# First product of the second layer in seven block products instead of eight

## The chip, the cores and the metric

The kernel runs on one core of one Trainium2 chip. A core has TensorE (matrix products, PE in the rows; its weight loads are listed apart as PEld), VectorE (DVE), ScalarE (ACT), GpSimd (POOL), SyncE (SP) and 16 DMA engines. Each engine works its own instructions in the order of the program and waits for others on semaphores. The metric is the device time of one execution in microseconds; the median of three runs stands for a kernel.

## The reference

Three layers follow each other, in float32: a decayed attention without softmax, a mixture of experts (each of 2304 tokens goes to 2 of 8 experts), and a dense layer, the "second layer" of the change:

```python
def _moe2_ref(x, w_in, w_out):          # x 2304 x 512, w_in 512 x 2048, w_out 2048 x 512
    h = x @ w_in
    relu6 = np.clip(h + 3.0, 0.0, 6.0)
    g = h * relu6 / 6.0
    return (g @ w_out).astype(np.float32)

def reference(**kwargs):
    attn_out = _attn_ref(**attn_kwargs)
    x = attn_out.transpose(0, 2, 1, 3).reshape(B * S, H * D)
    x = _moe_ref(x=x, **moe_kwargs)
    return _moe2_ref(x=x, **moe2_kwargs)
```

## The kernel before

Tokens go in 18 tiles of 128. All products are made in a type of TensorE with fewer bits (`F32R`): every operand is split into a high part, copied by ScalarE, and a low part, the rest, subtracted by VectorE. A product is then three passes, high by high, low by high, high by low, which accumulate in PSUM. `wstep` (L544 and L545) makes the splits of weights, `turn` (L643 to L646) transposes a tile of tokens on VectorE and splits it.

The expert stage (`moe`, about 116 to 564 us) runs in ten sweeps: single, single, six double ones, single, single. A sweep has 8 steps f. Each step makes first products `g1` (L690) into a PSUM tile `ga` or `gb`, ScalarE and VectorE make the high and low part of the hidden tile (L742, L743), and `flush` then issues the second product `g2` (L701) of the step before; so a hidden tile has the length of one step to be made. `w_in` and `w_out` come in a form of 8 bytes per number and are converted in 64 chunks during the sweeps from the third on (`cv_load`, `cv_run`, `cv_store`); the result goes to DRAM (`win`, `wout`). Results of experts go to DRAM (`yd`).

The second layer (`moe2`) takes the tiles in the groups of `GR` (L809): two, two, two, three, three, three, three. A group has 16 steps f, two per weight unit of 256 columns of `w_in` (8 units). A step has 12 matmuls of `g1` with 256 or 384 token columns, the four steps of `glu` (L879 to L882: relu on ScalarE, multiply on VectorE, high part on ScalarE, low part on VectorE), and the `g2` of the step before, three matmuls of 512 columns per tile. After a group's last `g2`, `o_out` (L894) copies its sums out. The split weights of both products are held in SBUF for the whole layer (four buffers `big` per unit).

`x2_prep` makes the tokens of the next group meanwhile: GpSimd gathers two rows of `yd` per token (L818), `x2_mix` adds them with their gates (L826, L827), the tile goes to DRAM and comes back in blocks (L635), and `turn` makes `self.x2`.

The order on each engine is that of the program text. SyncE issues the loads and stores in order, and an issue whose buffer isn't free, or whose data isn't ready, holds those behind it.

Of the kernel before, what the change touches and what calls it, by code (L numbers as in the profile page):

```python
# [64 lines left out]
class K:  # L65
# [437 lines left out]
    def w_load(self):  # L503
# [23 lines left out]
    def w_split(self):
# [4 lines left out]
        h1, l1 = self.big([P, 4, 256], F32R), self.big([P, 4, 256], F32R)  # L532
        h2, l2 = self.big([P, 2, DM], F32R), self.big([P, 2, DM], F32R)
        self.w[n] = (h1, l1, h2, l2)
        for j, (a, b) in enumerate(self.wst.pop(n)):
            s = slice(2 * j, 2 * j + 2)
            self.wq.append((n, h1[:, s], l1[:, s], a))
            self.wq.append((n, h2[:, j], l2[:, j], b))
# [174 lines left out]
    def moe(self, xs0):  # L713
# [3 lines left out]
        for si, sw in enumerate(self.SW):  # L717
# [5 lines left out]
            for f in range(8):  # L723
                n = e * 4 + f // 2
                cur = e * 4 if si in (0, len(self.SW) - 2) else n
                if f % 2 == 0:
                    if self.wsp <= cur + 4:
# [28 lines left out]
                self.prev = (w, fi, [(*s, a) for s, a in zip(subs, accs)], f == 0, f == 7)  # L756
# [52 lines left out]
    GR = [(0, 2), (2, 2), (4, 2), (6, 3), (9, 3), (12, 3), (15, 3)]  # L809
# [19 lines left out]
    def x2_prep(self, gi, f):  # L829

        if gi >= len(self.GR) or f < 0:
            return
        t0, G = self.GR[gi]
        if f == 0:
            self.ys = {}
            self.x2 = (self.act_t([P, 4, 384]), self.act_t([P, 4, 384]))
        step, mix, get, cut = ((0, 2, 4, 5), (3, 4, 6, 8), (3, 4, 6, 8), (2, 4, 6, 8), (3, 3, 5, 7))[min(gi, 4)]
        for j in range(G):
            rows = self.x2d[(t0 + j) * P:(t0 + j + 1) * P]
            if f == j * step:  # L840
                self.ys[j] = self.x2_gather(t0 + j)
            if f == j * step + mix:
                self.x2_mix(t0 + j, self.ys[j])
                self.nc.gpsimd.dma_start(rows, self.ys[j][0])  # L844
            if f == j * step + get:
                self.ys[j] = self.x_blocks(rows)
            if f == j * step + cut:
                c = slice(j * P, (j + 1) * P)
                self.turn(self.ys.pop(j), slice(0, P), self.x2[0][:, :, c], self.x2[1][:, :, c])()

    def moe2(self):
        for gi, (t0, G) in enumerate(self.GR):
            xs = self.x2
            acc = None
            for f in range(16):
                if f % 2 == 0:
                    if self.wsp <= 32 + f // 2 + 4:
                        self.w_split()
                    self.w_load()
                self.wstep(0, 32 + f // 2)  # L860
                w, fi = self.w[32 + f // 2], f % 2
                gh, gl = self.glu(w, fi, xs, G * P, "ga" if f % 2 == 0 else "gb")
                self.wstep()
                self.flush()
                if (gi, f) not in ((0, 7), (0, 11)):
                    self.wstep()
                if acc is None:
                    acc = [self.pacc([P, DM]) for _ in range(G)]
                self.prev = (w, fi, [(gh, gl, P, acc)], f == 0, f == 15)
                self.fin = (self.o_out, t0, acc)  # L870
                self.x2_prep(gi + 1, f - 1)
# [226 lines left out]
```

## Time and profile before

| what | value |
|---|---|
| median of 3 runs | 975.55 us (975.17 to 976.92) |
| the profiled execution: its time, its span | 976.63 us, 974.5 us |
| TensorE busy | 955.1 us, 98% of the span |
| VectorE, ScalarE, GpSimd busy | 535.4, 427.2, 202.6 us |
| moved by DMA | 138.80 MB, mean 142 GB/s |
| stages | attention to 116, experts to 564, second layer to the end |

The span is the time from the first to the last instruction of the trace, and the execution's own time is a little longer. A printed duration of a run of matmuls holds the end of the pipeline, so that two runs overlap; the distance from start to start is what a run costs. In the rows `x12` behind a shape is the number of instructions, and `[2.39 <-DVE h L743]` is the idle time ahead and what ended it.

### The profile page before, as it was taken

To read this page: it belongs to the slowest core of one execution; us is meant where nothing else is said; L and a number is where in the kernel's file an instruction comes from. 1 tells how busy PE (TensorE), PEld (TensorE's weight loads), DVE (VectorE), ACT (ScalarE), POOL (GpSimd) and SP (SyncE) were. 2 spreads that over 40 slices of the span, in tenths; PEclk is the share of its full clock that TensorE was granted. 3 is DMA by queue.
4 is the path that set the end of the run, shared out by engine and by line. 5 is a ranking of instruction groups with operands and counts; after the bars stand their busy time and mean duration, and the time that the engine had idled before them with its cause. 6 is when DMAs were issued, how large, how long until landed. Compare 5 with 4: busy or idle time off the path is not lost.

```text
span 974.5 us, 16460 instructions
## 1 busy us (share of the span) xinstructions
PE 955.1 (98%) x6056; PEld 855.6 (88%) x6056; DVE 535.4 (55%) x1219; ACT 427.2 (44%) x908; POOL 202.6 (21%) x277
## 2 busy tenths in 40 slices
PE   8999799999999999999999999999999999999997
PEld 6888688898989898988889889999999999999995
DVE  5688654776868677676843475343434334334222
ACT  4566424645445464645443474343423333333322
POOL 1245332232424232332410221011112021020000
PEclk9999899999999999999999999999999999999999
DMA  9774736884848577584432752122213022030001
GB/s 338 254 268 166 256 111 213 275 255 146 250 134 253 173 221 214 177 238 154 120 116 79 236 198 81 44 66 79 73 44 87 33 69 62 33 87 23 33 1 36
DMA packets 106184, 138.80 MB, mean 142 GB/s; under 512 B 10469, under 2 KB 66533, under 8 KB 106093
## 3 DMA queue, kind: packets, MB, share of 16 engines
q1 hardware_dynamic: 97821, 111.03, 36.4%
q0 software_dynamic: 7984, 26.10, 7.8%
q8 instruction: 49, 0.80, 0.3%
q10 hardware_dynamic: 288, 0.52, 0.1%
q14 instruction: 42, 0.34, 0.1%
HBM read 97.90 MB, written 39.71 MB: 141 GB/s over the span
## 4 chain that ended last, share of the span: by engine, by line
PE 94%; DVE 3%; issue 1%; DMA 1%; ACT 1%; another core or an unknown queue 0%; SPq 0%; DVEq 0%; ACTq 0%
PE p L701 42%; PE ga L690 23%; PE gb L690 20%; PE sc L192 2%; PE px L214 1%; PE p L175 1%; PE px L204 1%; DVE b L545 1%; PE p L253 1%; PE p L238 1%; DMA s<-xe 1%; PE p L112 1%; DVE b L194 0%; PE p L264 0%
## 5 line engine op out<-in xcount | busy, mean ns | idle before, releaser
L701 PE MATMUL p<-b,h 128*128 128x512 f32 (+1 forms) x1824 | 451.5, 393 | 0.0
L701 PEld LDWEIGHTS p<-b,h 128*128 128x128 f32 (+1 forms) x1824 | 329.9, 186 | 65.4 <-DVE h L882 0.5
L690 PE MATMUL ga<-x,b 128*128 128x360 f32 (+2 forms) x1344 | 234.2, 323 | 3.0 <-DVE h L743 2.4
L690 PEld LDWEIGHTS ga<-x,b 128*128 128x128 f32 x1344 | 222.0, 190 | 13.2 <-DVE h L743 2.8
L690 PE MATMUL gb<-x,b 128*128 128x384 f32 (+2 forms) x768 | 128.8, 316 | 0.0
L690 PEld LDWEIGHTS gb<-x,b 128*128 128x128 f32 x768 | 122.8, 189 | 5.2
L545 DVE TENSOR_TENSOR b<-b,b 128x512 fp32r<-128x512 f32 x128 | 93.2, 765 | 9.7 <-ACT b L544 9.3
L593 POOL TENSOR_TENSOR cvl<-cvl,cvs 128x256 f32<-128x256 f32 x64 | 47.4, 741 | 237.4 <-ACT cva L574 197.4
L690 PE MATMUL gb<-b,b 128*128 128x256 f32 x672 | 90.0, 283 | 0.0
L882 DVE SCALAR_TENSOR_TENSOR h<-h,h 128x384 fp32r<-128x384 f32 (+1 forms) x112 | 56.2, 502 | 61.1 <-ACT h L881 59.7
L690 PEld LDWEIGHTS gb<-b,b 128*128 128x128 f32 x672 | 87.2, 190 | 1.2
L881 ACT ACTIVATE h<-h 128x384 fp32r<-128x384 f32 (+1 forms) x112 | 53.7, 479 | 66.1 <-DVE h L880 64.4
L880 DVE SCALAR_TENSOR_TENSOR h<-h,ga 128x384 f32<-128x384 f32 (+1 forms) x56 | 27.8, 496 | 88.0 <-ACT h L879 87.9
L743 DVE SCALAR_TENSOR_TENSOR h<-gb,h 128x256 fp32r<-128x256 f32 (+1 forms) x64 | 27.8, 434 | 83.9 <-PE p L701 62.2
L544 ACT ACTIVATE b<-b 128x512 fp32r<-128x512 f32 x128 | 73.8, 623 | 0.0
L880 DVE SCALAR_TENSOR_TENSOR h<-h,gb 128x384 f32<-128x384 f32 (+1 forms) x56 | 27.8, 496 | 83.1 <-ACT h L879 81.9
L879 ACT ACTIVATE h<-ga,three 128x384 f32<-128x384 f32 (+1 forms) x56 | 29.9, 534 | 89.4 <-PE ga L690 89.2
L844 POOL DMA_DIRECT2D x2d<-s x18 | 10.4, 580 | 262.8 <-DVE s L827 262.8
L879 ACT ACTIVATE h<-gb,three 128x384 f32<-128x384 f32 (+1 forms) x56 | 30.0, 536 | 77.2 <-PE gb L690 74.7
L645 ACT ACTIVATE x<-xp 128x512 fp32r<-128x512 f32 (+1 forms) x39 | 22.8, 584 | 75.1 <-DVE xp L643 74.0
L594 POOL TENSOR_TENSOR cvl<-cvt,cvl 128x256 f32<-128x256 f32 x64 | 52.9, 827 | 5.0
L742 ACT ACTIVATE h<-gb 128x256 fp32r<-128x256 f32 (+1 forms) x64 | 25.3, 395 | 64.0 <-PE gb L690 55.2
(143 smaller groups left out, 895.9 us busy)
## 6 DMA issues: line engine op xcount, KB each, us to landing
b<-in_moe_w_dram SPq DMA_DIRECT2D x64, 512.0 KB
s<-xe SPq DMA_DIRECT2D x140, 64.0 KB
s<-in_moe_w_in_dram SPq DMA_DIRECT2D x32, 256.0 KB
s<-in_moe_w_out_dram SPq DMA_DIRECT2D x32, 256.0 KB
yd<-s SPq DMA_DIRECT2D x24, 240.0 KB
b<-in_k_dram SPq DMA_DIRECT2D x18, 256.0 KB
b<-in_q_dram SPq DMA_DIRECT2D x18, 256.0 KB
b<-in_v_dram SPq DMA_DIRECT2D x18, 256.0 KB
```

The source lines that it names most:

```text
L544: self.nc.scalar.activation(h, a, AF.Copy)
L545: self.nc.vector.tensor_sub(l, a, h.bitcast(F32))
L593: nc.gpsimd.tensor_mul(lf, lf, s.bitcast(F32))
L594: nc.gpsimd.tensor_add(lf, t.bitcast(F32), lf)
L690: nc.tensor.matmul(p, a[:, k, f], b[:, k, :n], start=(i == 0), stop=(i == 11))
L701: nc.tensor.matmul(a[:R], x[:, c], y[:, fi, :], start=(first and i == 0), stop=(last and i == 2))
L742: nc.scalar.activation(hh, p, AF.Relu)
L743: nc.vector.scalar_tensor_tensor(hl, p, 0.0, hh.bitcast(F32), op0=OP.max, op1=OP.subtract)
L879: nc.scalar.activation(r, p, AF.Relu, bias=self.three)
L880: nc.vector.scalar_tensor_tensor(r, r, 6.0, p, op0=OP.min, op1=OP.mult)
L881: nc.scalar.activation(gh, r, AF.Copy, scale=1.0 / 6.0)
L882: nc.vector.scalar_tensor_tensor(gl, r, 1.0 / 6.0, gh.bitcast(F32), op0=OP.mult, op1=OP.subtract)
```

## The change

The first product of the second layer is made for four tiles and two column blocks of `w_in` at once by Strassen's scheme: with the weight unit cut into 2 x 2 blocks and the tokens into 2 x 2 blocks, seven block products replace eight, and sums of weight blocks, of token blocks and of products take the place of the eighth. The groups become two, four, four, four, four. The first group keeps the plain form.

- *Sums of weights.* From the fourth sweep on, `pr_step` works one of 64 jobs per step (two in the last sweep): a load of a unit of `w_in`, four sums on VectorE (L924 to L928), four splits of 512 columns (L933 on ScalarE, L934 on VectorE), four stores to DRAM (`wc`). `w_in` is no longer held in SBUF; the look-ahead of the weight splits goes from 4 to 3 units in most sweeps, and all chunks of `w_in` are converted ahead of those of `w_out`.
- *Stream.* `wc_load` reads the pieces back from `wc` on SyncE: two of 512 KB per unit in the first group, three and a half per unit in every other one.
- *Rounds.* `g1_seven` makes per unit seven products of six matmuls of 256 columns into four PSUM tiles (`ga`, `gb`, `tp` and one more). Two tiles take more than one product, and ScalarE copies a partial result before the next one is added. Four copies on ScalarE and four sums on VectorE give two tiles of 512 hidden columns; `hidden` does for them what `glu` did.
- *Tokens.* `x2_prep` transposes tiles into `raw2`, `x2_sums` makes four sums on VectorE, and `x2_set` splits the seven operands: one ahead, six at the last round of a group.

```diff
-    GR = [(0, 2), (2, 2), (4, 2), (6, 3), (9, 3), (12, 3), (15, 3)]
+    GR = [(0, 2), (2, 4), (6, 4), (10, 4), (14, 4)]
...
-                    if self.wsp <= cur + 4:
+                    if self.wsp <= cur + (3 if 1 < si < 8 else 4):
...
+                if si > 2:
+                    self.pr_step(2 if si == len(self.SW) - 1 else 1)
                 if si == len(self.SW) - 1:
                     self.x2_prep(0, f - 1)
+                    if f in (5, 7):
+                        self.wc_load(f // 7)
...
+    def x2_sums(self):
...
+        v.tensor_sub(t3, b22, b12)
+        v.tensor_sub(b12, b12, b11)
+        v.tensor_sub(t2, b22, b12)
+        v.tensor_sub(t4, t2, b21)
+        self.x2f = {1: b11, 2: b21, 3: b22, 4: t4, 5: b12, 6: t2, 7: t3}
...
+    def x2_set(self, *names):
...
+            nc.scalar.activation(x[:, 0], f, AF.Copy)
+            nc.vector.tensor_sub(x[:, 1], f, x[:, 0].bitcast(F32))
...
+        def split(i, n):
+            o[i] = self.big([P, 2, 2, 2, P], F32R)
+            h, l = o[i][:, :, 0], o[i][:, :, 1]
+            nc.scalar.activation(h, t[n], AF.Copy)
+            v.tensor_sub(l, t[n], h.bitcast(F32))
...
+        yield load
+        yield lambda: sums("s")
+        yield lambda: sums("d")
+        yield lambda: split(0, "a1")
+        yield lambda: both(1, "s")
+        yield lambda: both(2, "d")
+        yield lambda: both(3, "a2")
+        yield lambda: store(3)
...
+    def plain(self, t0, G):
...
+                self.wc_load(p + 2 if p < 6 else p + 1)
...
+            gh, gl = self.glu(self.wcs[p][fi], self.x2, G * P, "ga" if fi == 0 else "gb")
+            if f == 15:
+                self.x2_set(2, 5, 6, 4, 3, 7)
...
+    def seven(self, gi, t0, G):
...
+        for p in range(8):
+            self.wc_load(gi * 8 + p + 1)
+            c = self.g1_seven(X, self.wcs.pop(gi * 8 + p))
+            if p == 7 and gi + 1 < len(self.GR):
+                self.x2_set(2, 5, 6, 4, 3, 7)
+            h = [self.hidden(x) for x in c]
+            self.flush()
...
+            self.x2_prep(gi + 1, 2 * p - 1)
+            self.x2_prep(gi + 1, 2 * p)
...
+        mul(a, 1, True, False)
+        c1 = copy(a, "cva")
+        mul(b, 2, True, True)
+        v.tensor_add(h0[:, 0:n], b, c1)
+        mul(d, 5, True, False)
+        c5 = copy(d, "cvl")
+        mul(a, 6, False, False)
+        c2 = copy(a, "cvt")
+        mul(c, 4, True, True)
+        c4 = copy(c, "cvl")
+        mul(d, 3, False, True)
+        v.tensor_add(h0[:, n:], d, c2)
+        mul(a, 7, False, True)
+        v.tensor_sub(h1[:, 0:n], a, c4)
+        v.tensor_add(h1[:, n:], a, c5)
...
+    def hidden(self, x):
...
+        nc.scalar.activation(r, x, AF.Relu, bias=self.three)
+        v.scalar_tensor_tensor(x, r, 6.0, x, op0=OP.min, op1=OP.mult)
+        h = self.big([P, 2, DM], F32R)
+        nc.scalar.activation(h[:, 0], x, AF.Copy, scale=1.0 / 6.0)
+        v.scalar_tensor_tensor(h[:, 1], x, 1.0 / 6.0, h[:, 0].bitcast(F32), op0=OP.mult, op1=OP.subtract)
+        return h
```

**TensorE, second layer.** In the rows `p_...` are PSUM tiles, `h_...` hidden tiles, `x_...` tokens, `b_...` weights. Before, one step of a group of three tiles:

```order
L690 MATMUL ga<-x_9136,b_7242 128x384 x4
L690 MATMUL ga<-x_9136,b_7243 128x384 x4
L690 MATMUL ga<-x_9137,b_7242 128x384 x4
L701 MATMUL p_9630<-b_7172,h_9960 128x512
L701 MATMUL p_9630<-b_7173,h_9960 128x512
L701 MATMUL p_9630<-b_7172,h_9961 128x512
L701 MATMUL p_9631<-b_7172,h_9960 128x512
```

Now, the first round of the second group (`mga`, `mgb`, `mtp` and `p_7825` are the four tiles of the products, in the order 1, 2, 5, 6, 4, 3, 7):

```order
L1037 MATMUL mga<-b_7768,b_7734 128x256 x6
L1037 MATMUL mgb<-x_7791,b_7734 128x256 x6
L1037 MATMUL p_7825<-x_7794,b_7736 128x256 x6
L1037 MATMUL mga<-x_7797,b_7736 128x256 x6
L1037 MATMUL mtp<-x_7800,b_7740 128x256 x6
L1037 MATMUL p_7825<-b_7803,b_7738 128x256 x6
L1037 MATMUL mga<-b_7806,b_7738 128x256 x6
L707 MATMUL p_7285<-b_7473,h_7771 128x512
```

Twelve matmuls ahead of a second product became 42; the fourth and seventh set of six write the tile of the first one, the sixth that of the third.

**ScalarE, end of a group of the second layer.** Before, L879 and L881 (`glu`) go on without a break, and the output copies L894 stand behind them:

```order
L879 ACTIVATE h_9052<-gb,three 128x384
L881 ACTIVATE h_9037<-h_9052 128x384
L879 ACTIVATE h_9081<-ga,three 128x384
L881 ACTIVATE h_9066<-h_9081 128x384
L894 ACTIVATE s_9095<-p_8578 128x512
L894 ACTIVATE s_9098<-p_8579 128x512
```

Now, from the last copy of the eighth round of a group (L1042) to the first two copies of the next group's first round:

```order
L1042 ACTIVATE mc<-mtp 128x256
L897 ACTIVATE x_8663<-b_8133 128x512
L897 ACTIVATE x_8666<-b_8367 128x512
L897 ACTIVATE x_8669<-s_8585 128x512
L897 ACTIVATE x_8672<-s_8587 128x512
L897 ACTIVATE b_8675<-b_8367 128x512
L897 ACTIVATE b_8678<-s_8586 128x512
L1067 ACTIVATE s_8681<-s_8607,three 128x512
L1070 ACTIVATE b_8684<-s_8607 128x512
L1067 ACTIVATE s_8687<-s_8608,three 128x512
L1070 ACTIVATE b_8690<-s_8608 128x512
L1042 ACTIVATE mc<-mga 128x256
```

The six splits of the next group's tokens (L897) stand between the copies of a round and the hidden tiles of that round (L1067, L1070).

**VectorE, end of the last sweep.** Before, the two transposes of the first group's tokens (L643, L646) come behind splits of weights (L545):

```order
L545 TENSOR_TENSOR b_6999<-s_6920,b_6998 128x512
L545 TENSOR_TENSOR b_7001<-s_6922,b_7000 128x512
L643 STREAM_TRANSPOSE xp<-s_6988 128x4x4x32
L646 TENSOR_TENSOR x_6829<-xp,x_6828 128x4x128
L643 STREAM_TRANSPOSE xp<-s_6993 128x4x4x32
L646 TENSOR_TENSOR x_6829<-xp,x_6828 128x4x128
L743 SCALAR_TENSOR_TENSOR h_7049<-gb,h_7048 128x360
```

Now:

```order
L545 TENSOR_TENSOR b_7149<-s_7063,b_7148 128x512
L545 TENSOR_TENSOR b_7149<-s_7065,b_7148 128x512
L934 TENSOR_TENSOR b_7185<-s_7099,b_7185 128x2x256
L934 TENSOR_TENSOR b_7189<-s_7128,b_7189 128x2x256
L643 STREAM_TRANSPOSE xp<-s_7134 128x4x4x32
L646 TENSOR_TENSOR x_6971<-xp,x_6970 128x4x128
L643 STREAM_TRANSPOSE xp<-s_7139 128x4x4x32
L646 TENSOR_TENSOR x_6971<-xp,x_6970 128x4x128
L749 SCALAR_TENSOR_TENSOR h_7201<-gb,h_7200 128x360
L934 TENSOR_TENSOR b_7227<-b_7097,b_7227 128x2x256
```

Two splits of weight sums (L934) came ahead of the transposes, and the last one stands behind them.

## Rows read from the trace of the kernel before

**Rows 1.** The page's span, TensorE's busy share, the chain by engine.

```profile
span 974.5 us, 16460 instructions
...
PE 955.1 (98%) x6056; PEld 855.6 (88%) x6056; DVE 535.4 (55%) x1219; ACT 427.2 (44%) x908; POOL 202.6 (21%) x277
...
PE 94%; DVE 3%; issue 1%; DMA 1%; ACT 1%; another core or an unknown queue 0%; SPq 0%; DVEq 0%; ACTq 0%
```

**Rows 2.** Windows (a sweep, two groups): PE, PEld, DVE, ACT, POOL, clock, DMA, GB/s.

```profile
393.00:448.00 55.00, 55.00 (x313) 49.33 (x312) 40.34 (x86) 27.92 (x65) 16.82 (x22) 1.00 0.68 203
...
569.70:614.90 45.20, 45.20 (x290) 41.04 (x289) 26.47 (x53) 24.46 (x52) 9.60 (x10) 1.00 0.40 132
...
838.00:905.00 67.00, 67.00 (x339) 60.98 (x338) 24.05 (x41) 23.12 (x42) 5.59 (x7) 1.00 0.17 54
```

**Rows 3.** Timeline of TensorE, group of two tiles: start, duration, instructions.

```profile
571.71 1.60 PE L690 MATMUL gb<-x,b 128*128 128x256 f32 x12
573.15 1.55 PE L701 MATMUL p<-b,h 128*128 128x512 f32 x6
574.54 1.60 PE L690 MATMUL ga<-x,b 128*128 128x256 f32 x12
```

**Rows 4.** Timeline of TensorE and ScalarE, group of three tiles.

```profile
956.53 2.27 PE L690 MATMUL ga<-x,b 128*128 128x384 f32 x12
...
958.63 2.22 PE L701 MATMUL p<-b,h 128*128 128x512 f32 x9
958.83 0.58 ACT L879 ACTIVATE h<-ga,three 128x384 f32<-128x384 f32 x1 [2.44 <-PE ga L690]
...
960.70 2.27 PE L690 MATMUL gb<-x,b 128*128 128x384 f32 x12
```

**Rows 5.** Weight loads of the first product by shape: busy us, mean ns.

```profile
L690 PEld LDWEIGHTS gb<-x,b 128*128 128x128 f32 x768 | 122.8, 189 | 5.2
```

**Rows 6.** Instructions of ScalarE and VectorE by shape: busy us, mean ns.

```profile
L742 ACT ACTIVATE h<-gb 128x256 fp32r<-128x256 f32 x56 | 21.5, 384 | 46.2 <-PE gb L690 41.1 <-PE p L701 5.1
...
L544 ACT ACTIVATE b<-s 128x512 fp32r<-128x512 f32 x32 | 18.6, 621 | 0.0
...
L826 ACT ACTIVATE s<-s,gw 128x512 f32<-128x512 f32 x18 | 12.7, 710 | 0.0
...
L894 ACT ACTIVATE s<-p 128x512 f32<-128x512 f32 x17 | 9.1, 590 | 1.3 <-PE p L701 1.2
...
L743 DVE SCALAR_TENSOR_TENSOR h<-gb,h 128x256 fp32r<-128x256 f32 x56 | 23.6, 422 | 74.1 <-PE p L701 62.2 <-ACT h L742 11.9
...
L545 DVE TENSOR_TENSOR b<-s,b 128x512 fp32r<-128x512 f32 x32 | 20.9, 688 | 5.4 <-ACT b L544 4.3
...
L827 DVE SCALAR_TENSOR_TENSOR s<-s,gw,s 128x512 f32<-128x512 f32 x18 | 13.5, 751 | 2.8 <-DMA s<-yd,slotc 1.5 <-ACT s L826 0.8
```

**Rows 7.** Timeline of TensorE in the first sweeps, and a window of it.

```profile
176.03 3.56 PE L690 MATMUL ga<-x,b 128*128 128x360 f32 x12 [2.39 <-DVE h L743]
...
189.11 2.14 PE L690 MATMUL ga<-x,b 128*128 128x360 f32 x12
...
176.00:177.00 1.00, 0.97 (x3) 0.97 (x4) 1.00 (x2) 0.23 (x1) 0.00 (x0) 0.50 0.93 324
```

**Rows 8.** Timeline of the ninth sweep and the last: loads, second product, a gather.

```profile
512.31 5.76 SPq L635 DMA_DIRECT2D s<-xe  x12
...
518.08 1.55 PE L701 MATMUL p<-b,h 128*128 128x512 f32 x6
...
542.12 1.46 POOL L818 DMA_INDIRECT s<-yd,slotc  x1 [0.30 <-issue]
...
548.93 0.75 DVE L827 SCALAR_TENSOR_TENSOR s<-s,gw,s 128x512 f32<-128x512 f32 x1 [1.52 <-DMA s<-yd,slotc]
```

**Rows 9.** Timeline at the start of the second layer.

```profile
562.36 0.69 DVE L646 TENSOR_TENSOR x<-xp,x 128x512 fp32r<-128x512 f32 x1 [0.67 <-ACT x L645]
...
562.58 1.59 PE L690 MATMUL ga<-x,b 128*128 128x256 f32 x12
```

**Rows 10.** Windows of 5 us with the busiest DMA, early and in the second layer.

```profile
15.00:20.00 5.00, 5.00 (x70) 4.69 (x70) 2.56 (x5) 2.81 (x6) 0.00 (x0) 1.00 1.05 400
572.00:577.00 5.00, 5.00 (x34) 4.56 (x34) 4.00 (x8) 3.74 (x8) 3.90 (x4) 1.00 1.03 364
```

More of the change, by code (lines that the diff above doesn't have):

```diff
@@ L536, in w_split @@
             s = slice(2 * j, 2 * j + 2)
[L537 removed]
+            if n < 32:
+                self.wq.append((n, h1[:, s], l1[:, s], a))
             self.wq.append((n, h2[:, j], l2[:, j], b))
@@ L689, in g1, with parts @@
             for k in range(4):
-                nc.tensor.matmul(p, a[:, k, f], b[:, k, :n], start=(i == 0), stop=(i == 11))
+                nc.tensor.matmul(p, a[k], b[:, k, :n], start=(i == 0), stop=(i == 11))
                 i += 1
         return p
+    @staticmethod
+    def parts(w, fi):
+        f = slice(fi * P, (fi + 1) * P)
+        return [[w[u][:, k, f] for k in range(4)] for u in range(2)]
     def g2(self, w, fi, subs, first, last):
@@ new lines, in x2_prep @@
+        if gi and s == begin[-1] + cut + 1:
+            self.x2_sums()
+        if gi and s == begin[-1] + cut + 2:
+            self.x2s = {}
+            self.x2_set(1)
+    def x2_sums(self):
+        v = self.nc.vector
+        r0, r1 = (r.rearrange("p (h k) n -> p h (k n)", h=2) for r in self.raw2)
+        b11, b21, b12, b22 = r0[:, 0], r0[:, 1], r1[:, 0], r1[:, 1]
+        t2, t3, t4 = (self.row([P, DM]) for _ in range(3))
+        v.tensor_sub(t3, b22, b12)
[3 more added lines that the diff above has]
+        self.x2f = {1: b11, 2: b21, 3: b22, 4: t4, 5: b12, 6: t2, 7: t3}
@@ new lines, in x2_set, with pr_init @@
+    def x2_set(self, *names):
+        nc = self.nc
+        for n in names:
+            x = self.big([P, 2, DM], F32R) if n in (1, 3, 7) else self.act_t([P, 2, DM])
+            f = self.x2f[n]
+            nc.scalar.activation(x[:, 0], f, AF.Copy)
+            nc.vector.tensor_sub(x[:, 1], f, x[:, 0].bitcast(F32))
+            self.x2s[n] = x.rearrange("p l (k n) -> p l k n", k=2)
+    def pr_init(self):
+        self.wc = self.dr.tile([8, 4, P, 1024], F32, name="wc")
+        self.pq = [j for p in range(8) for j in self.pr_jobs(p)]
+        self.wcn, self.wcs = 0, {}
@@ L851, in moe2 @@
     def moe2(self):
         for gi, (t0, G) in enumerate(self.GR):
[L853 to L871, printed above, removed]
@@ new lines, in g1_seven, with mul, copy @@
+    def g1_seven(self, X, W):
+        nc, v = self.nc, self.nc.vector
+        n = 2 * P
+        a, b, c = (self.ps.tile([P, n], F32, name="m" + t, tag=t) for t in ("ga", "gb", "tp"))
+        d = self.pacc([P, n])
+        def mul(t, s, first, last):
+            w, x = W[s], X[s]
+            for i, (k, u, z) in enumerate([(k, u, z) for u, z in ((0, 0), (1, 0), (0, 1)) for k in range(2)]):
+                nc.tensor.matmul(t, w[:, u, k], x[:, z, k], start=(first and i == 0), stop=(last and i == 5),
+                                 skip_group_check=True)
+        def copy(t, tag):
+            o = self.sb.tile([P, n], F32, name="mc", tag=tag, bufs={"cva": 2, "cvt": 2, "cvl": 3}[tag])
+            nc.scalar.activation(o, t, AF.Copy)
+            return o
+        h0, h1 = self.row([P, 2 * n]), self.row([P, 2 * n])
+        mul(a, 1, True, False)
[13 more added lines that the diff above has]
+        v.tensor_add(h1[:, n:], a, c5)
+        return h0, h1
@@ L876, in glu @@
         gh, gl = self.hid([P, n]), self.hid([P, n])
-        p = self.g1(w, fi, xs, n, tag)
+        p = self.g1([[w[:, k // 2, u, k % 2] for k in range(4)] for u in range(2)], xs, n, tag)
         r = self.hid([P, n], F32)
```

145 lines of the change are left out of this document (116 added, 29 removed).

## The prediction

> **What bounds the kernel now.** I read the page's head first: TensorE is busy 98% of the 974.5 us span and 94% of the chain that ended last is TensorE [rows 1]. So a change must shorten TensorE's own row of work, and everything else matters only where it lets TensorE stand. Then the stages: in the second layer (570 to 972) TensorE is busy in every microsecond while VectorE and ScalarE have half or more of theirs free, and the DMA share is 0.40 in the first group and 0.17 late [rows 2]. In the expert stage VectorE has 40.3 of 55.0 us and the DMA 0.68 at 203 GB/s [rows 2]. Last, the timeline of TensorE in a group of two tiles and in one of three: a first product (12 matmuls) and a second product (6 or 9) alternate without a gap [rows 3, 4]. The profiled execution took 976.63 us, 2.1 more than its span; the median is 975.55, and I take differences from the median.
>
> **TensorE's work.** A start-to-start distance is the true price, since the printed durations overlap. Two-tile group: 12 matmuls of 256 columns take 573.15 - 571.71 = 1.44 us, 0.120 each; 6 of 512 take 1.39, 0.232 each [rows 3]. Three-tile group: 12 of 384 take 2.10, 0.175 each; 9 of 512 take 2.07 [rows 4]. The first two tiles keep the old form. The other 16 stood in two groups of two and four of three, 16 first products each: 32 x 1.44 + 64 x 2.10 = 180.5 us. Strassen makes 4 groups x 8 units = 32 rounds of 7 x 6 = 42 matmuls of 256 columns: 1344 x 0.120 = 161.3. That is **-19.2 us**. A bare count of columns (7 of 8) would give 22.6; the rest goes because 256 columns cost 0.120 where two thirds of 0.175 is 0.117. The second product keeps its 864 matmuls: 0.
>
> Weight loads: 192 more of them, 189 ns each [rows 5]. They lie beside the matmuls already, for the spacing of 0.120 [rows 3] is below one load's 0.189: 0. The Trainium skill ("TensorE: Matmul & The Clock Gate", Part 3, The mechanism) lets a load run beside a matmul in flight only when the row groups differ. By that rule 192 loads would add 192 x 0.19 = 36 us; the trace speaks against it by the same two numbers.
>
> **ScalarE and VectorE in a steady round.** Let T be the end of a round on TensorE. Then 24 second-product matmuls take 5.54 us, and the next round's fourth product adds onto the first one's accumulator, so ScalarE's copy c1 must have ended by T + 5.54 + 3 x 0.72 = T + 7.70. A copy of 256 columns is 0.39, of 512 0.62, a scaled 512 one 0.71; VectorE's 512-wide steps are 0.69 to 0.75 [rows 6]. The four `hidden` steps of ScalarE alternate with four of VectorE; as an estimate ScalarE is free at T + 4.4, with a mix (0.71) at T + 5.1. c1 could start as late as T + 7.3: 2.2 us spare, **0**.
>
> **Where ScalarE is late.** `x2_set` puts six copies on ScalarE and six subtractions on VectorE ahead of `hidden`, at each group's last round. ScalarE: six copies to T + 2.87, first relu to 3.58. VectorE: subtractions to 5.20, then the first multiply to 5.89. From there each waits for the other: copy 6.51, relu 7.22, multiply 7.91, copy 8.53, c1 8.92 against 7.70. Three such boundaries at 1.2 to 1.4: **3.9**. From group 0 to 1 the flush is only 6 matmuls, and the six copies stand before c1: two steps of the plain product to 1.5, copies to 5.24, c1 to 5.63, and TensorE wants it at 1.39 + 3 x 0.72 = 3.55: **2.1**. In group 1's first round the flush is again only 1.39 us, with two output copies of 0.59 [rows 6] behind `hidden` on ScalarE: c1 of the next round ends at 5.98 against 3.55: **2.4**. Sum 8.4. Bounds: half of it, if TensorE's other three products reach further than I let them, and 11, if each VectorE step also waits for a semaphore's 0.2 us (the gap between TensorE's end and ScalarE's start at 958.63 and 958.83 [rows 4]).
>
> **The clock.** After TensorE stood 2.39 us at 173.6, its next 12 matmuls took 3.56 instead of 2.14 at a granted clock of 0.50, that is 1.2 GHz: 1.42 lost [rows 7]. Five waits of 1.2 to 2.4 us come in; only the longest is as long as that row's. I take one loss, **+1.4**; bounds 0 and five times 1.4.
>
> **The expert stage.** Eight jobs per unit: four 256-wide sums (0.43 each) and four splits. VectorE rises by 4 x 0.43 + 4 x 0.69 = 4.5 us per sweep to 44.8 of 55.0; the DMA by one load and four stores of half a megabyte, 2.6 MB per 55 us, to 251 GB/s [rows 2]. Both stay below full, and TensorE's second product is always one step behind: 0, with a bound of 2 in the sweeps. In the single sweep after 503 a sums job waits on VectorE for a weight load that SyncE issues only after five stores and four of the twelve `xe` loads (at about 514.3) [rows 8]. Queued behind the waiting sums stands the low half of the hidden tile, which TensorE wants two matmuls after 518.08, at 518.5 [rows 8]. The nearest landing is a gather's: issued until 543.6, there at 548.9, 5.3 us [rows 8]. By that the low half would be 2.4 late; if half a megabyte lands in 3 us, 0. I take **+1.0**.
> The shorter look-ahead of the weight splits (3 units for 4) takes nothing from TensorE while a sweep of 55.0 us takes four units and a unit's splits need 8 steps on two engines; what leaves (the w_in splits, 8 steps per unit before and in group 0) was beside TensorE and gives nothing back.
> Before group 0, VectorE's last split of the input ends 563.05, after TensorE's first product began at 562.58, so there is no slack [rows 9]; now two splits for the sums (0.69 each) stand ahead of the two transposes: **+1.3**, bounds 0 and 1.4.
>
> **The DMA of group 0.** The last store of sums waits for a split at about 565.8, and SyncE is in order: the pieces of units 1 to 7 are queued behind it. Up to unit 5's pieces that makes 2.1 MB of stores, 5.2 of pieces, 1.6 of w_out and 1.8 of gathers: 10.7 MB in the 25.5 us to 591.3, when TensorE wants them. The busiest windows of before moved 364 GB/s (in this stage) and 400 (early, plain loads) [rows 10]; that is 3.9 and 1.2 us late. I take **+2.5**, bounds 0.5 and 7 (at 329 GB/s, which this stage would give if gathers and stores mix worse). The Trainium skill ("DMA: Bandwidth & Descriptors", Where 436 GB/s comes from) puts the limit for one core at about 358 GB/s; by it the lag is 4.4 and the sum 972.9. The row of 400 stands above that figure.
> Later groups stream 1.8 MB per unit of 10.58 us, 174 GB/s, beside some 60 [rows 2], and stay one unit ahead: 0. At the very end the last output copy follows the last second product as before: 0.
>
> **Sum:** -19.2 + 8.4 + 1.4 + 1.0 + 1.3 + 2.5 = -4.6, so 975.55 - 4.6 = **971.0** (a profiled run like the one before would show about 972).
>
> **Rivals.** *ScalarE and VectorE keep up better*: waits of 4.2 in all, no clock loss, group 0 lag 0.5, si 8 at 0: -19.2 + 4.2 + 0.5 + 1.3 = -13.2, 962.3. For it: both engines have half their time free in this stage [rows 2]. Against it: they go in program order, and the six copies stand before what TensorE waits for.
> *The clock falls at all five waits*: 4 x 1.4 more, 976.6, no change. For it: the one wait of this kind did it [rows 7]. Against: four of the five are shorter than that row's.
> *Slower: the stream of group 0 is no faster than the expert stage's.* That stage moved 203 GB/s at a busy share of 0.68, 299 when full [rows 2], and its mix of rows and stores is nearer to this one than the plain loads. Then unit 5's pieces are 10.3 late in place of 2.5: +3.2, 978.8. It decides from about 310 GB/s downward. Against it: 364 GB/s in this very stage [rows 10].
> *The loads are not hidden*: 192 loads of 0.189 [rows 5] would cost 36 and make it 1007; as good as excluded, since 0.120 [rows 3] is less than one load.
> *It does not do what it says*: some order or buffer I read wrongly holds TensorE in every round. One microsecond in each of 32 rounds would undo the gain.
>
> **How the numbers follow.** Forecast 971.0, with its own range 968 to 974: 0.52. Better: 0.13. Clock at all waits: 0.14. Slow stream: 0.14. Loads not hidden 0.01, the unread hold 0.06. The range goes from the better case to the slow stream, 962.5 to 979.0, and leaves the ends out. A measurement of this kernel tells about 0.2% (2 us) from no change. Faster: 0.13 + nearly all of 0.52, less its upper end 0.02 = 0.63. Same: 0.02 + the clock's 0.14 + a little of the others, 0.18. Slower: 0.19.
>
> **What would show it.** Rounds of 42 matmuls in 5.04 us (0.120 each); 10.6 us from unit to unit within a group; TensorE idle 1.2 to 2.4 us before the fourth product at the four boundaries, released by ScalarE's copy; one stretch at 0.50 in the granted clock near 620; DMA near its full share from 566 to about 600, with TensorE waiting for `wc` pieces around unit 5. Matmuls above 0.125, or a wait in steady rounds, or no wait at boundaries, would make the forecast wrong.

## The result and the profile after

The changed kernel takes 981.33 us (median of 7, 979.51 to 984.57) against 975.48: a ratio of 1.0066, 95% interval 1.0049 to 1.0083. It is slower by 0.7%; 971.0 was forecast. TensorE's work in the later groups shrank about as computed, and more than that came back, as time in which it stands or runs at the lower clock. The head of the page of the changed kernel, which answers to [rows 1]:

```profile
span 979.1 us, 17572 instructions
...
PE 943.3 (96%) x6248; PEld 836.7 (85%) x6248; DVE 608.4 (62%) x1359; ACT 472.9 (48%) x1000; POOL 204.7 (21%) x277
...
PE 77%; DVE 9%; DMA 5%; ACT 3%; issue 3%; SPq 1%; another core or an unknown queue 0%; DVEq 0%; ACTq 0%
```

TensorE is busy 11.8 us less, but its share of the chain that ended last fell from 94% to 77%. The windows of the changed kernel, in the columns of [rows 2], are a sweep, group 0 (the first group of the second layer, in the plain form) and a stretch of the later groups:

```profile
393.00:448.00 55.00, 54.96 (x311) 48.74 (x310) 44.87 (x94) 29.24 (x68) 18.03 (x22) 1.00 0.79 250
...
570.00:616.00 46.00, 39.28 (x232) 34.56 (x231) 19.57 (x39) 19.07 (x40) 12.32 (x14) 0.93 0.88 307
...
820.00:860.00 40.00, 40.00 (x255) 36.42 (x254) 19.93 (x37) 18.19 (x35) 8.00 (x10) 1.00 0.77 255
```

The sweep carries what was counted (VectorE 44.9, 250 GB/s). The later groups are full. In group 0 TensorE stands 6.7 of 46 us, and the clock is down for a part of it. What TensorE waited for in the changed kernel (total, times, longest):

```profile
PE p L707 <- ACT h L1081: 9.4, 4, 5.2
PE mga L1037 <- ACT mc L1042: 4.2, 5, 1.9
PE p L707 <- DVE h L749: 2.9, 2, 1.8
...
PE ga L690 <- DMA b<-wc: 1.0, 1, 1.0
```

The first line is new and stands in group 0 alone. The second holds the five waits that were forecast, at half their size. The last one is the wait that the forecast had put the loss of group 0 on.

The stages compare best by the starts of TensorE's runs: the first one of 360 columns in the double sweeps, the last of them, the first of the last sweep, of group 0 and of group 1, and the end of the last second product (in the changed kernel 174.31, 499.53, 532.41, 568.13, 629.28 and 972.69). The distances in us, for the profiled execution of each kernel:

| kernel | double sweeps | ninth | last | group 0 | groups 1 to 4 |
|---|---|---|---|---|---|
| before | 323.2 | 31.6 | 31.8 | 45.9 | 358.8 |
| changed | 325.2 | 32.9 | 35.7 | 61.2 | 343.4 |
| e1_pieces_once | 327.6 | 33.8 | 34.7 | 46.0 | 343.7 |
| e2_sums_early | 329.4 | 34.2 | 31.9 | 53.1 | 343.4 |
| e3_load_ahead | 325.1 | 31.6 | 32.9 | 60.0 | 345.1 |
| e4_mix_later | 326.8 | 34.0 | 34.7 | 51.9 | 349.0 |
| e5_raw_group0 | 326.1 | 32.9 | 36.3 | 52.7 | 343.6 |
| e6_no_sums_work | 322.9 | 31.6 | 31.8 | 62.0 | 343.4 |
| e7_combined | 324.6 | 31.6 | 32.6 | 50.4 | 343.6 |
| e9_pieces_behind_stores | 326.2 | 33.0 | 36.3 | 54.5 | 343.7 |
| e10_no_gathers | 326.0 | 33.2 | 35.3 | 48.2 | 345.2 |
| e11_combined_later | 323.8 | 31.6 | 32.7 | 52.3 | 344.8 |

Groups 1 to 4 gave 15.4 us; group 0 alone took 15.3 back, the last sweep 3.9, the double sweeps 2.0, the ninth 1.3. (The start of the double sweeps lies between 172.7 and 177.9 in these profiles and follows no edit. Changed, e1, e4, e9 and e10 have the same jobs in their sweeps, and still differ by up to 2.4 us in the double ones, 1.1 in the ninth and 1.7 in the last. All of them lie above the kernel before, but a difference of that size between two of them tells nothing.)

**What TensorE waits for in group 0.** The timeline of the changed kernel from SyncE's stores to TensorE, the longest of the waits:

```profile
562.43 7.76 SPq L937 DMA_DIRECT2D wc<-b  x4
...
574.80 1.32 SPq L717 DMA_DIRECT2D yd<-s  x3
...
584.86 1.00 POOL L829 DMA_INDIRECT s<-yd,slotc  x1 [30.97 <-DVE b L545]
...
591.55 0.72 ACT L837 ACTIVATE s<-s,gw 128x512 f32<-128x512 f32 x1 [3.69 <-DMA s<-yd,slotc]
592.18 0.46 ACT L1079 ACTIVATE h<-gb,three 128x256 f32<-128x256 f32 x1
...
593.11 0.75 DVE L838 SCALAR_TENSOR_TENSOR s<-s,gw,s 128x512 f32<-128x512 f32 x1 [4.52 <-DMA s<-yd,slotc]
...
594.69 2.93 PE L707 MATMUL p<-b,h 128*128 128x512 f32 x6 [5.21 <-ACT h L1081]
597.42 2.48 PE L690 MATMUL gb<-x,b 128*128 128x256 f32 x12
```

Read from below: TensorE stood 5.21 us for a hidden tile. Its relu (592.18) stands in ScalarE's order behind the mix of a tile of group 1 (591.55), and its multiply in VectorE's order behind the second half of that mix (593.11). The mixes waited 3.69 and 4.52 for gathers from `yd`. The first gather went out at 584.86, 16.7 us into the group (before: 9.6), when a row buffer came free from a split of `w_out`; the stores of `yd`, which it reads, had left SyncE at 574.80, behind four stores of weight sums, and shared the DMA with the pieces. A second wait of this kind, 3.19 us at 623.5, came from a transpose that waited for blocks read back:

```profile
622.00 0.71 DVE L871 STREAM_TRANSPOSE b<-s 128x512 f32<-128x512 f32 x1 [4.33 <-DMA s<-x2d]
...
623.52 2.93 PE L707 MATMUL p<-b,h 128*128 128x512 f32 x6 [3.19 <-ACT h L1081]
```

The 15.3 us are 10.35 of waits (0.98, 0.53, 5.21, 0.44, 3.19), 3.7 of low clock after the two long ones (from 594.69 and from 623.52 to the same runs at full clock), and some 1.2 that these don't explain.

### The profile page after: what moved, and what is told of

The parts are those of the page before. It is cut to its first block, busy times and chain, and to the rows that moved or that the text cites. A ratio compares the mean times of both kernels' runs of the same rounds, so it can differ in the third digit from the quotient of the medians.

```text
span 979.1 us, 17572 instructions
## 1 busy us (share of the span) xinstructions
PE 943.3 (96%) x6248; PEld 836.7 (85%) x6248; DVE 608.4 (62%) x1359; ACT 472.9 (48%) x1000; POOL 204.7 (21%) x277
## 4 chain that ended last, share of the span: by engine, by line
PE 77%; DVE 9%; DMA 5%; ACT 3%; issue 3%; SPq 1%; another core or an unknown queue 0%; DVEq 0%; ACTq 0%
PE p L707 35%; PE ga L690 11%; PE gb L690 9%; PE mga L1037 7%; PE p L1037 4%; PE mtp L1037 2%; PE mgb L1037 2%; DVE b L545 2%; PE sc L192 1%; PE px L214 1%; DMA s<-wout 1%; PE p L175 1%; PE px L204 1%; SPq L635 1%; DVE cvt L588 1%
## 5 line engine op out<-in xcount | busy, mean ns | idle before, releaser
L707 PE MATMUL p<-b,h 128*120 128x512 f32 (+1 forms) x1056 | 264.7, 398 | 12.3 <-ACT h L1081 9.4
L707 PEld LDWEIGHTS p<-b,h 128*120 128x120 f32 (+1 forms) x1056 | 190.1, 186 | 56.1 <-ACT h L1081 10.2
L707 PE MATMUL p<-b,b 128*128 128x512 f32 x768 | 180.0, 390 | 0.0
L707 PEld LDWEIGHTS p<-b,b 128*128 128x128 f32 x768 | 142.2, 188 | 28.2
L690 PE MATMUL ga<-x,b 128*128 128x360 f32 (+1 forms) x768 | 135.5, 325 | 4.3 <-DVE h L749 2.4
L690 PEld LDWEIGHTS ga<-x,b 128*128 128x128 f32 x768 | 125.9, 190 | 14.0 <-DVE h L749 7.0
L545 DVE TENSOR_TENSOR b<-b,b 128x512 fp32r<-128x512 f32 x128 | 85.6, 706 | 12.2 <-ACT b L544 11.7
L1071 DVE SCALAR_TENSOR_TENSOR b<-s,b 128x512 fp32r<-128x512 f32 x64 | 44.3, 693 | 44.7 <-ACT b L1070 44.7
L1070 ACT ACTIVATE b<-s 128x512 fp32r<-128x512 f32 x64 | 40.5, 632 | 57.8 <-DVE s L1068 56.1
L749 DVE SCALAR_TENSOR_TENSOR h<-gb,h 128x256 fp32r<-128x256 f32 (+1 forms) x64 | 27.7, 433 | 59.4 <-PE p L707 46.7
L1067 ACT ACTIVATE s<-s,three 128x512 f32<-128x512 f32 x64 | 45.8, 716 | 23.6 <-DVE s L1057 23.6
L1037 PE MATMUL mga<-b,b 128*128 128x256 f32 x384 | 56.3, 282 | 0.0
L1037 PEld LDWEIGHTS mga<-b,b 128*128 128x128 f32 x384 | 52.6, 191 | 2.5
L1042 ACT ACTIVATE mc<-mga 128x256 f32<-128x256 f32 x64 | 24.5, 383 | 54.4 <-PE mga L1037 51.2
```

The costliest lines, as they stand in the source:

```text
L545: self.nc.vector.tensor_sub(l, a, h.bitcast(F32))
L690: nc.tensor.matmul(p, a[k], b[:, k, :n], start=(i == 0), stop=(i == 11))
L707: nc.tensor.matmul(a[:R], x[:, c], y[:, fi, :], start=(first and i == 0), stop=(last and i == 2))
L749: nc.vector.scalar_tensor_tensor(hl, p, 0.0, hh.bitcast(F32), op0=OP.max, op1=OP.subtract)
L1037: nc.tensor.matmul(t, w[:, u, k], x[:, z, k], start=(first and i == 0), stop=(last and i == 5), skip_group_check=True)
L1067: nc.scalar.activation(r, x, AF.Relu, bias=self.three)
```

## The experiments

Theories on group 0: **A**, the order of SyncE's queue (stores of sums and pieces ahead of what the tokens need); **B**, the volume of the pieces; **C**, the place of mixes and transposes; later **F**, that only the tokens' chain is late, against **G**, the step of the prediction, that the pieces themselves are late. On the sweeps: **D**, VectorE's added work and order, against **E**, the added DMA traffic. Ratios are to the kernel before, measured beside each run: 976.94 us for e1 to e4, 976.85 for e5, e6, e7 and e9, 973.04 for e10 and e11. So totals of different sets compare by their ratios.

**e1_pieces_once**

```diff
-                self.wcs[n] = [self.wc_tile(p, i) for i in (0, 3)]
+                self.wcs[n] = [self.wc_tile(p, i) for i in (0, 3)] if p == 0 else self.wcs[0]
```

> Group 0 uses the pieces of weight unit 0 for all eight units (so the first two tiles are wrong), which leaves out 14 loads of 512 KB; all else stays. The first group takes 61.2 us in the changed kernel and 45.9 before. Theory A (queue): SyncE is held by the last four stores of sums until 569.8, so w_out loads come late, rows come free late, and gathers are issued at 584.9 in place of 572; without the pieces the w_out loads come some 2 to 3 us earlier and land faster, group 0 about 55, total about 975. Theory B (volume): the pieces fill the DMA (340 to 411 GB/s from 565 to 595) and that alone makes the gathers late; group 0 about 47.5, total about 967.5.

970.34 us, ratio 0.9939 (0.9926 to 0.9953). Group 0 takes 46.0 as before, the first mix comes at 15.5 us into it and waits for nothing. Without the pieces the whole loss of group 0 is gone, though the stores of sums are still there, which speaks for B. But the edit takes 14 loads out of SyncE's queue with the bytes, so by itself it doesn't tell queue from volume.

**e2_sums_early**

```diff
-                    self.pr_step(2 if si == len(self.SW) - 1 else 1)
+                    self.pr_step(2 if si in (7, 8) else 1)
```

(and the loads ahead as in the next one)

> Two jobs of sums per step in the eighth and ninth sweep, none in the last; each load of a unit stands half a unit ahead of its sums. The last stores of sums are then out before the last sweep. Theory A (queue): SyncE is free at the start of group 0, gathers at about 575, group 0 about 48, and the stall of 1.84 us with its 1.8 us of low clock in the last sweep is gone: total about 965. Theory B (volume): only 2.1 MB less after 566, some 6 us at 350 GB/s, and the last sweep's 3.7: total about 972.

977.18 us, 1.0003 (0.9987 to 1.0018). The last sweep is back at 31.9 and group 0 falls to 53.1: by 8.1 us, where A wanted 13 and B some 6. But the sweeps pay: with two jobs in a step VectorE comes late, and TensorE waits 0.56, 1.01, 0.41 and 2.33 us for the low halves that VectorE makes. The sums are not free.

**e3_load_ahead**

```diff
+        for p in range(1, 8):
+            early, job = q[p][0], q[p - 1][4]
+            q[p][0] = lambda: None
+            q[p - 1][4] = lambda early=early, job=job: (early(), job())
```

> Only the load of each weight unit stands half a unit ahead of its sums; jobs and stores stay where they are. Both theories: the stall of VectorE in the ninth sweep (1.05 us of TensorE) and in the last (1.84 and 1.8 of low clock) go, 4.7 us. Theory A: the last split of sums, and with it SyncE, comes some 4 us earlier too, but group 0 starts as much earlier, so its 61 us stay: total about 976.6. Theory B the same. If the stall stays, its cause is not the load behind which the sums stand.

980.21 us, 1.0038 (1.0024 to 1.0051). The ninth sweep is exactly as before, 31.55, the last loses 1.1 in place of 3.9, group 0 stays. So the sums that wait for their load are the cause of the stalls in these two sweeps, as predicted for the ninth. The total is above the 976.6 expected, in part because in this profile groups 1 to 4 take 1.7 us longer, at the lower clock behind one wait (see the last section).

**e4_mix_later**

```diff
-        begin, mix, get, cut = (((0, 0), 2, 4, 5), ((0, 1, 3, 4), 3, 5, 7), ((0, 2, 4, 6), 2, 3, 4))[min(gi, 2)]
+        begin, mix, get, cut = (((0, 0), 2, 4, 5), ((0, 1, 3, 4), 4, 6, 8), ((0, 2, 4, 6), 2, 3, 4))[min(gi, 2)]
```

(and `x2_set(1)` in the step of `x2_sums` for this group)

> The mixes, reads back and transposes of the second group's tokens stand one step (2.8 us) later in group 0. Theory C (place): it is the place of mix and transpose in the order of ScalarE and VectorE, ahead of the hidden tile, that hands a late gather on to TensorE: the wait of 5.2 us falls by 2.8 and that of 3.2 goes or falls by as much, the low clock after one of them goes: total about 975. Theories A and B: the same direction, as the gathers are late for their own reasons; if the whole chain only shifts (gathers wait for rows that the later mixes free) the total stays at 981.

981.16 us, 1.0042 (1.0022 to 1.0061). Group 0 falls by 9.3, and groups 1 to 4 rise by 5.6: their first products now wait for tokens, which makes 1.2 us of waits more, and the clock is lower behind them and again in the second round. The total stays near that of the changed kernel, not at C's 975. So the place mostly passes the wait on; by these stages 3.7 of the 9.3 us were gained. The line of this kernel that shows the wait, at the start of group 1:

```profile
627.34 0.50 PE L1037 MATMUL mga<-b,b 128*128 128x256 f32 x2 [1.40 <-DVE b L898]
```

**e5_raw_group0**

```diff
+                self.raw0[n] = self.big([P, 4, 256])
+                self.nc.sync.dma_start(self.raw0[n], wi[:, :, p * 256:(p + 1) * 256])
...
+        self.nc.scalar.activation(t[:, :, 0], a, AF.Copy)
+        self.nc.vector.tensor_sub(t[:, :, 1], a, t[:, :, 0].bitcast(F32))
```

> Only group 0 differs from the changed kernel: it reads a unit of w_in as it is (512 KB) and splits it on chip, two steps of ScalarE and two of VectorE per unit, instead of reading two ready pieces (1 MB). Group 0 took 61.2 us in the changed kernel, 46.0 with the pieces read once, 45.9 before. Theory B (volume): 3.7 MB less in some 25 us, so gathers land some 8 to 10 us earlier and most of the loss goes: group 0 at 47 to 51, total 967 to 972. Theory A (what counts is the queue of SyncE, with the same number of issues less seven): group 0 stays above 55, total above 975.

977.7 us, 1.0008 (0.9990 to 1.0026). Group 0 at 52.7: half the bytes give back somewhat over half of the loss, short of what B promised. The splits of the first unit also made group 0 begin later: TensorE waits 2.96 us for one ahead of it (36.3 for the last sweep).

**e9_pieces_behind_stores**

```diff
-                self.wc_load(p + 2 if p < 6 else p + 1)
...
             self.flush()
+            if fi == 0:
+                self.wc_load(p + 2 if p < 6 else p + 1)
```

> In group 0 the loads of pieces stand behind the flush of the step, so behind the stores of the last experts' results, from which the gathers read. Theory A (queue): the stores go out and the gathers read some 3 us earlier, the wait of 5.2 us falls by that: total about 976. Theory B (volume): the pieces come 3 us later, the gathers share the DMA with them as before; total 979 to 983.

979.14 us, 1.0022 (1.0006 to 1.0039). Same bytes, other order: group 0 at 54.5. The first gather comes at 14.6 us in place of 16.7, and now TensorE does wait for pieces (2.4 us). The total lies in the range of B, but the bytes are the same and group 0 is 6.7 us shorter, so order counts beside volume; B alone falls.

**e6_no_sums_work**

```diff
         def sums(i):
+            return
...
         def split(i, n):
+            return
...
-            nc.sync.dma_start(self.wc[p, i], o.pop(i).rearrange("p s l k f -> p (s l k f)").bitcast(F32))
+            nc.sync.dma_start(self.wc[p, i], t["a"].rearrange("p k f -> p (k f)"))
```

> The jobs load and store as before, but the four sums and four splits are left out (the raw unit is stored four times, so the output is wrong): no work on VectorE and ScalarE in the sweeps, the same DMA traffic. The six double sweeps (first to last first product of 360 columns) took 325.2 us against 323.2 before, the ninth sweep 32.9 against 31.6, the last 35.7 against 31.8. Theory D (VectorE's order): 323.3, 31.6, 31.9, total about 973.5 with group 0 still at 60. Theory E (DMA traffic slows the sweeps): 325, with the ninth and last at 31.6 and 32.

977.43 us, 1.0007 (0.9993 to 1.0020). The window of a sweep of this kernel, beside the one of the changed kernel above:

```profile
393.00:448.00 55.00, 55.00 (x312) 49.20 (x311) 40.06 (x86) 27.86 (x64) 16.68 (x23) 1.00 0.82 250
```

The same 250 GB/s, VectorE at 40.06 as before, TensorE busy throughout; sweeps 322.9, ninth 31.6, last 31.8, group 0 about as in the changed kernel at 62.0. E falls and D holds in the main: with the same traffic the loss ahead of group 0 is gone but for some 0.5 us in the double sweeps. The edit takes out ScalarE's splits as well, so in the double sweeps it doesn't tell VectorE's work from ScalarE's; in the ninth sweep and the last it is VectorE's order that the waits name (`DVE h L749`). The total fell less than the stages, as the double sweeps began 3.2 us later than in the changed kernel.

**e10_no_gathers**

```diff
-            if s == b:
+            if s == b and gi != 1:
                 self.ys[j] = self.x2_gather(t0 + j)
-            if s == b + mix:
+            if s == b + mix and gi != 1:
```

(and `rows` of tiles 0 and 1)

> The changed kernel without the gathers, mixes and stores of the second group's four tiles during group 0: the blocks of tiles 0 and 1 are read in their place (so those four tiles are wrong). The pieces of group 0 are streamed as in the changed kernel. Theory F (the tokens): the pieces themselves come in time; what TensorE waits for is the hidden tile, whose steps stand behind mixes and transposes that wait for late gathers: group 0 at 46 to 49 (61.2 in the changed kernel), total about 968. Theory G (the recorded step): the pieces themselves are late at TensorE, 10.7 MB by unit 5; without gathers only 1.8 MB of it goes, group 0 at 52 or more and most waits for loads of pieces.

971.56 us, 0.9979 (0.9962 to 0.9996). All pieces are streamed, and group 0 takes 48.2. In group 0 of this kernel two waits are left, of 1.15 and 0.29 us, and none for a piece; the longer one:

```profile
582.78 1.65 PE L707 MATMUL p<-b,h 128*128 128x512 f32 x6 [1.15 <-ACT h L1082]
```

F holds, and G's 52 or more falls: 13 of the 15.3 us go with the tokens' chain. It runs from the stores of the last experts over gathers, mixes, stores and reads back to the transposes. The pieces are the other half of the cause: without them the same chain cost nothing (e1), and without the chain's gathers and mixes the same pieces cost 2.3 us. What e10 doesn't test is the lateness of 2.5 us that the prediction took: by its own sum the 8.9 MB without the gathers need 24.5 us at 364 GB/s and are in time. (The total is above the 968 expected in part because the clock fell in the second round here too, groups 1 to 4 at 345.2.)

**e7_combined**: raw units in group 0 as in e5, loads ahead as in e3, and

```diff
-                if si > 2:
+                if si > 2 or si == 2 and f > 1:
                     self.pr_step(2 if si == len(self.SW) - 1 else 1)
```

> Group 0 from raw units as in e5_raw_group0, loads of units half a unit ahead as in e3_load_ahead, and the jobs start one sweep earlier (third sweep, third step), so that the last stores of sums are out after the fifth step of the last sweep. Theory B: sweeps 325, ninth 31.6, last 32, group 0 at 46 to 48, groups 1 to 4 at 343.4: total about 962. Theory A the same if the queue is free then; if group 0 stays above 52, neither volume nor stores were it.

968.03 us, 0.9905 (0.9889 to 0.9922): faster than both kernels. The page of this kernel:

```profile
span 966.1 us, 17629 instructions
...
PE 939.1 (97%) x6248; PEld 835.6 (86%) x6248; DVE 626.0 (65%) x1375; ACT 480.0 (50%) x1016; POOL 209.5 (22%) x277
```

Sweeps, ninth and last came out as expected (324.6, 31.6, 32.6); group 0 did not: 50.4 for 46 to 48. The first mix still comes at 17.8 us into the group and waits 1.3 for a gather.

**e11_combined_later**: e7 with the loads behind the flush, mixes one step later and the sums of tokens spread over two steps.

> e7_combined (968.0; group 0 at 50.4) with three more edits in group 0: loads of raw units behind the flush, so behind the stores of the last results; the mixes of the second group one step later, reads back and transposes where they were; the four sums of tokens spread over two steps. Theory F: the waits of 0.72 and 0.21 before mixes and of 1.57 behind the sums go, group 0 at 47 to 48.5, total about 966. If the gathers only shift with the rows, group 0 stays at 50 and the total at 968.

967.08 us beside 973.04 for the kernel before in the same job, 0.9939 (0.9924 to 0.9953): no better than e7. The first mix no longer waits, but group 0 is at 52.3 with more and later waits (1.45, 1.59). They stand behind transposes that waited for blocks read back, 1.17 us and 2.93 us (at 606.54); the first of them:

```profile
595.58 0.71 DVE L874 STREAM_TRANSPOSE b<-s 128x512 f32<-128x512 f32 x1 [1.17 <-DMA s<-x2d]
```

How the last 4 us of group 0 go is left open. So is the share of queue and volume in what slows the chain: stores out earlier (e2), half the bytes (e5) and another order (e9) each give back 6.7 to 8.5 of the 15.3 us, and e7, which has the first two, 10.8.

Where the tokens of group 1 are, in us after the start of group 0, and the length of the group:

| kernel | stores of `yd` | first gather | first mix | group 0 |
|---|---|---|---|---|
| before | 4.1 | 9.6 | 18.8 | 45.9 |
| e1_pieces_once | 4.2 | 11.2 | 15.5 | 46.0 |
| e7_combined | 5.1 | 10.5 | 17.8 | 50.4 |
| e5_raw_group0 | 7.0 | 12.5 | 19.7 | 52.7 |
| e2_sums_early | 4.1 | 11.0 | 17.6 | 53.1 |
| e9_pieces_behind_stores | 4.5 | 14.6 | 20.9 | 54.5 |
| changed | 6.7 | 16.7 | 23.4 | 61.2 |

The kernel before mixed only two tiles in this group, the first in the sixth step (in the order of the program), and neither waited. The others have four, the first in the fifth step. Among those, the later the first mix, the longer the group, e2 excepted. (The first gather doesn't order them: e1 gathers later than e7 and has the shorter group.)

## Why the prediction was wrong

**TensorE's work, -19.2: right.** A round and a unit of the changed kernel:

```profile
644.50 5.63 PE L707 MATMUL p<-b,b 128*128 128x512 f32 x24
649.97 0.88 PE L1037 MATMUL mga<-b,b 128*128 128x256 f32 x6
650.68 0.88 PE L1037 MATMUL mgb<-x,b 128*128 128x256 f32 x6
...
655.00 5.18 PE L707 MATMUL p<-b,b 128*128 128x512 f32 x22
```

Six matmuls of 256 columns lie 0.71 to 0.72 apart, 0.120 each, weight loads hidden; a unit takes 655.00 - 644.50 = 10.50 (10.58 forecast, the second product's 24 in a row being a little faster than taken). Groups 1 to 4 came out 15.4 shorter, which is -19.2 with the 4.2 of waits, within 0.4. No steady round waited, as forecast.

**ScalarE late at the boundaries, +8.4: right in mechanism, mis-sized; it was 4.2**, the lower bound (0.93 and 1.88 in the first two rounds, 0.45 at three boundaries). Changed kernel, first boundary of groups of four:

```profile
708.44 1.28 DVE L898 TENSOR_TENSOR x<-b,x 128x512 fp32r<-128x512 f32 x2
708.69 0.62 ACT L897 ACTIVATE b<-b 128x512 fp32r<-128x512 f32 x1
709.21 0.62 ACT L897 ACTIVATE b<-s 128x512 fp32r<-128x512 f32 x1
...
712.05 0.68 DVE L1068 SCALAR_TENSOR_TENSOR s<-s,s 128x512 f32<-128x512 f32 x1
...
715.73 0.98 PE L1037 MATMUL mga<-x,b 128*128 128x256 f32 x6 [0.45 <-ACT mc L1042]
```

Six subtractions took 712.05 - 708.44 = 3.61, 0.60 each, where I had 0.69; two copies start 0.52 apart, where I had 0.62. The sum went by printed durations on these two engines and by distances of starts on TensorE alone. Instructions of ScalarE and VectorE overlap too.

**Clock, +1.4 in the second round: not in this profile.** None of the five waits lowered it here; in e3, e4 and e10 the same wait in the second round did, for 1.5 us each (last section), so the term stood for something that comes and goes. In the changed kernel the clock fell after the waits of 1.84, 5.21 and 3.19 in the last sweep and group 0, at 1.8, 2.2 and 1.5 us.

**Sweeps, 0 with a bound of 2: 2.0 by the table, and 2.9 at like clock.** The first 12 matmuls of these sweeps ran at the lower clock in the kernel before [rows 7] and at the full one here. From the next run of 360 columns on (182.24 before, 179.68 now) the sweeps took 316.98 and 319.85 us, which is above the bound. The added work was not free: without it (e6) 0.5 of the 2.9 is left.

**Ninth sweep, +1.0: right.** 1.3 by the stage, one wait of 1.05, by the mechanism given:

```profile
514.72 0.39 SPq L915 DMA_DIRECT2D b<-win  x1
...
518.82 0.43 DVE L924 TENSOR_TENSOR s<-b 128x256 f32<-128x256 f32 x1 [3.61 <-DMA b<-win]
...
519.62 0.42 DVE L749 SCALAR_TENSOR_TENSOR h<-gb,h 128x256 fp32r<-128x256 f32 x1
...
520.10 1.19 PE L707 MATMUL p<-b,h 128*128 128x512 f32 x4 [1.05 <-DVE h L749]
```

**Before group 0, +1.3: it was 3.9.** I counted the two splits ahead of the transposes (e3, which has only them, loses 1.1). I didn't ask the ninth sweep's question again here, where two jobs stand in one step, and a load and its sums with them: SyncE issues at 551.47, split and sums start behind it at 559.2, and TensorE waits 1.84 (560.63) and then loses 1.8 at the lower clock.

```profile
551.47 0.40 SPq L915 DMA_DIRECT2D b<-win  x1
...
559.20 0.63 ACT L933 ACTIVATE b<-b 128x512 fp32r<-128x512 f32 x1 [4.37 <-DMA b<-win]
559.25 0.42 DVE L924 TENSOR_TENSOR s<-b 128x256 f32<-128x256 f32 x1 [4.58 <-issue]
```

**DMA of group 0, +2.5 (bounds 0.5 and 7): the step that failed; it was 15.3.** The rates were about as taken: 343 to 349 GB/s from 565 to 580 and 374 to 411 from there to 595, 372 on the mean, between the 364 and 400 of the sum. The last three of these windows of the changed kernel:

```profile
580.00:585.00 5.00, 4.47 (x27) 3.72 (x26) 2.36 (x5) 2.29 (x5) 0.14 (x1) 1.00 1.03 405
585.00:590.00 5.00, 4.49 (x32) 3.97 (x30) 1.23 (x3) 1.05 (x2) 3.74 (x4) 1.00 1.04 411
590.00:595.00 5.00, 0.31 (x1) 0.31 (x2) 1.41 (x3) 1.86 (x4) 0.58 (x1) 0.76 0.97 374
```

(The Trainium skill, "DMA: Bandwidth & Descriptors", Where 436 GB/s comes from, has about 358 GB/s as one core's limit; 405 and 411 stand above it.) The pieces held TensorE for 1.0 us, not 2.5, and those were unit 1's. At unit 5, where the sum had them late, TensorE came 6.7 us of waits later and found them there; whether they would have been late without those waits isn't shown. What failed is that the step asked only when TensorE's own operand lands. It named the stores that hold SyncE and the gathers as bytes, but did not follow what else was queued behind them and who waits for it: stores of `yd`, gathers, mixes and transposes, which stand in the order of ScalarE and VectorE ahead of hidden tiles that TensorE waits for: 9.4 of its 10.35 us of waits, and 13 of the 15.3 us by e10. The slower rival had the right stage and the wrong mechanism: it wanted a rate below 310 GB/s.

The parts add up: -15.4 + 2.0 + 1.3 + 3.9 + 15.3 = 7.1; the double sweeps of this profile began 1.7 earlier than those of [rows 7], which leaves the 5.4 between the two ends of TensorE's work (972.69 and 967.26).

## What to carry to other kernels

When a change adds traffic to a stage, list every transfer that shares the queue and the engines with it, and for each one the instruction that waits for it and what stands behind that instruction in its engine's order; the time may be lost behind another transfer than the one that was added. Here the added pieces held TensorE for 1.0 us, and the tokens' gathers and reads back, which they slowed, cost most of the rest. A saving in a full engine is worth what its feeders can follow, so the first group after a change of stage, where the pipeline is refilled, is to be counted by itself. Use distances of starts for every engine, not for TensorE alone.

## What the runs showed of the hardware

The clock did not fall by the length of a wait alone. At one and the same place TensorE stood 2.37 to 2.40 us in all twelve profiles; the 12 matmuls behind it took 3.5 to 3.8 us in six of them, the kernel before among them [rows 7], 2.24 or 2.25 in five, the changed one among them, and 2.76 in one:

```profile
174.31 2.25 PE L690 MATMUL ga<-x,b 128*128 128x360 f32 x12 [2.37 <-DVE h L749]
...
641.52 0.98 PE L1037 MATMUL mga<-x,b 128*128 128x256 f32 x6 [1.88 <-ACT mc L1042]
642.34 0.88 PE L1037 MATMUL mtp<-x,b 128*128 128x256 f32 x6
...
560.63 2.37 PE L707 MATMUL p<-b,h 128*120 128x512 f32 x7 [1.84 <-DVE h L749]
562.80 3.26 PE L690 MATMUL gb<-x,b 128*128 128x360 f32 x12
```

The wait of 1.88 at 641.5 left it up, the one of 1.84 at 560.6 took it down. In e3, e4 and e10 the same wait in the second round, 1.87 or 1.88 us, took it down as well. In e3 the granted clock is 0.51 from 638.5 to 641.5, where the changed kernel has 1.00 from 641.5 to 645:

```profile
638.01 1.19 PE L1042 MATMUL mga<-x,b 128*128 128x256 f32 x6 [1.88 <-ACT mc L1047]
639.00 1.48 PE L1042 MATMUL mtp<-x,b 128*128 128x256 f32 x6
```

What decides stayed open. And a load of half a megabyte needed 4.1 us from its issue to its first use in the ninth sweep (514.72 to 518.82), and in the last sweep the use came 7.7 us after the issue (551.47 to 559.20).
